# Attention, routed experts and a dense layer on one core: own PSUM for the first queries, gate exponentials moved, expert rows loaded twice, weight quarters in another order

## The chip, the core and the metric

One core of a Trainium2 chip runs the whole program. The metric is device time in microseconds, the median of the timed runs. The engines are named as the profile names them: PE (TensorE matmul), PEld (its weight load), DVE (VectorE), ACT (ScalarE), POOL (GpSimd) and SP (SyncE, which here only issues DMAs). A name with q behind it (SPq, ACTq) is the queue of that engine.

## What is computed

Three stages, each on the result of the one before, all in float32.

- Attention over 8 batches of 8 heads, 576 positions, 64 wide. `phi(x)` projects x to 128 features, subtracts the row's largest absolute value and takes `exp` of plus and minus the result (256 features). Then `num = phi(q) @ (phi(k).T @ v)` and `out = num / (phi(q) @ sum(phi(k)) + 1e-6)`.
- Routed experts over the 4608 tokens of 512. A token with `x @ w_skip <= 0` is passed through. The others go to the expert with the largest of 8 logits `x @ w_gate`; with the softmax weight of that expert, `out = x + gate * (relu(x @ w1[e]) @ w2[e])`, hidden width 1024.
- A dense layer: `h = x @ w_in` (2048 wide), `(h - tanh(h)) @ w_out`.

## The kernel before, in words

**Precision.** Matmuls of the expert and dense layers run in three passes: every operand is split into a high part (an ACT cast, line 96) and a low part (a subtraction, line 97, on DVE or POOL), and high*high, high*low and low*high are added up in PSUM.

**Attention (lines 664 to 796).** The loop over `i` has 32 steps, one for a pair of heads and one half of the positions of two batches. A step projects keys and queries of the next step (`project`, lines 233 to 249, into a PSUM tile `proj` of which the pool `pproj` has a single buffer), `shift`s them on DVE (line 255 reduces, line 259 subtracts, both reading `proj`), exponentiates (`exp_k` on ACT, line 266; `key_sum` adds them up on POOL, lines 278 to 281), transposes the shifted queries (`transpose_q`, line 287, PSUM tile `tq`), exponentiates these (`exp_q`, line 293), and forms key*value (`key_value`, line 306; `key_value_1`, line 320, from the key sums), its copy to SBUF (`keep_key_value`, ACT, line 312) and the numerators (`numerator`, line 344, PSUM tile `num`). As `proj` has one buffer, a projection waits until the `shift` of the projection before it has read the tile. Every engine runs its own instructions in the order in which the code issues them.

Before the loop (lines 664 to 696) step 0's keys and queries are done, with the first of the 16 words of the dense layer's `w_in` in between: `narrow` (line 194) turns a 64-bit word into float32 in four DVE operations and one or two on ACT and POOL (lines 198 to 217), `store_w` puts the result to DRAM, `load_words` loads the next word into the same place. In the loop a word is narrowed over two steps: lines 198 and 201 at the end of an even step, line 210 at the end of the odd one.

Routing runs eight steps behind, in phases (`phase = i % 8`): logits in phase 0, `route_pick` in 1, `route_gate` (lines 439 to 447: ACT exponentiates the logits, line 441, DVE sums them, line 443) and `route_rank` (DVE and POOL) in phase 2 at the end of the step, `route_count` in phase 3 (two small matmuls, then DVE lines 455 and 456).  Phase 2 comes three times in the loop; a fourth `route_gate` runs after it (line 867).

**Experts (lines 864 to 950).** Tokens are scattered to rows `xs` sorted by expert. Three tiles of 128 tokens are done early; the others in a loop whose step handles one tile (16 steps here), from a table `mt` in SBUF. SP reads row numbers, expert numbers and flags out of `mt` into registers (`values_load`, `entry`). A step computes `up` (two halves of the hidden width, each 12 matmuls with `w1`), relu on ACT (line 825), `relu_t` (four transposes and a split into `hh` and `hl`), `xtr(xt)` (the next tile's rows transposed and split into `xTh` and `xTl`), `down` (24 matmuls with `w2`, line 841), `gated` on DVE (line 848) and `out_row`, a store by SP. Three row tiles go round: `xr` holds this tile's rows (read by `gated`), `xt` the next one's (read by `xtr`), `xu` is being loaded; at the end of a step DVE copies `xt` to `xr` and `xu` to `xt` (lines 949 and 950).

Weights of one expert fill `raw[0]` (w1) and `raw[1]` (w2), 2 MB each, loaded by SP in two parts each (`load_part`). In the step where an expert's tiles begin (`first`), `raw[1]` is split in four quarters of 1024 columns (`wsplit(1, ...)`): ACT casts all, DVE subtracts quarters 0 and 2, POOL 1 and 3. Quarters 0 and 1 come ahead of `up(0, 0)`, quarters 2 and 3 right behind it. `down` uses quarter 0 for its first six matmuls, then 1, 2 and 3. In a step whose successor begins an expert (`nfirst`), `raw[0]` is split for the successor (`split_up`, lines 936 to 943). SP loads new weights into a part as soon as its splits have read it: `load_w(..., 1, ...)` at line 928 for `raw[1]`, lines 945 and 946 for `raw[0]`. After the last expert, `raw[0]` takes half of `w_in` in the same way.

**Dense layer (lines 954 to 1066).** Nine blocks of 512 tokens, gathered by indirect DMAs.

Of the kernel before, what the change touches and what calls it, by code (L numbers as in the profile page):

```python
# [8 lines left out]
F32 = mybir.dt.float32  # L9
# [6 lines left out]
PSUM = bass.MemoryType.PSUM  # L16
# [3 lines left out]
P = 128  # L20
# [39 lines left out]
def attention_moe_moe_kernel(  # L60
# [82 lines left out]
    ap = actx.enter_context(tc.tile_pool(name="att", bufs=1))  # L143
    sm = actx.enter_context(tc.tile_pool(name="small", bufs=2))
    pp = actx.enter_context(tc.tile_pool(name="pproj", bufs=1, space=PSUM))
    pt = actx.enter_context(tc.tile_pool(name="ptr", bufs=1, space=PSUM))
    pn = actx.enter_context(tc.tile_pool(name="pnum", bufs=1, space=PSUM))

    kvb = pk.tile([P, 512], F32, name="kvb")

# [6 lines left out]
    kf = [ap.tile([P, 2, 2, NF], F32, name=f"kf{j}") for j in range(2)]  # L157
    qp = [ap.tile([P, 2, NCH, P], F32, name=f"qp{h}") for h in range(2)]
    kvt = ap.tile([P, 2 * NF], F32, name="kvt")
    num = pn.tile([P, 2, 512], F32, name="num")[:, :, : NCH * VE].rearrange("p h (c w) -> p h c w", c=NCH)  # L160

    ko = kvb[:, K_T:].rearrange("p (s h w) -> p s h w", s=2, h=2)
    runb = rt.tile([P, E], F32, name="runb")
# [30 lines left out]
    def narrow(w, e, m, x, dve=False):  # L194

        w = w.rearrange("p (n t) -> p n t", t=2)
        low, high = w[:, :, 0].bitcast(U32), w[:, :, 1].bitcast(U32)
        nc.vector.tensor_scalar(  # L198
            out=e, in0=high, scalar1=0x7FF00000, scalar2=None, op0=ALU.bitwise_and
        )  # L200
        nc.vector.tensor_scalar(  # L201
            out=m, in0=high, scalar1=0xFFFFF, scalar2=None, op0=ALU.bitwise_and
        )
        yield
        nc.scalar.activation(e, e, AF.Relu, scale=8.0, bias=bias[:, 0:1])
        nc.scalar.activation(x, low, AF.Identity, scale=2.0**-32, bias=bias[:, 1:2])  # L206
        if not dve:
            nc.scalar.copy(m.bitcast(F32), m)
        yield
        nc.vector.scalar_tensor_tensor(  # L210
            out=e, in0=high, scalar=0x80000000, in1=e, op0=ALU.bitwise_and, op1=ALU.bitwise_or
        )
        if dve:
            nc.vector.tensor_tensor(out=x, in0=x, in1=m, op=ALU.add)  # L214
        else:
            nc.gpsimd.tensor_tensor(out=x, in0=x, in1=m.bitcast(F32), op=ALU.add)
        nc.gpsimd.tensor_tensor(out=x, in0=x, in1=e.bitcast(F32), op=ALU.mult)  # L217
        yield
# [11 lines left out]
    def blk(c, h):  # L230
        return 4 * h + c if c < 4 else 8 + h

    def project(i, w):


        src = st[i][w]
        p = st[i]["p" + w] = pp.tile([P, 12, NF], F32, name="proj")
        for c in range(4):
            for h in range(2):
                r = slice(h * DH, h * DH + DH)  # L240
                nc.tensor.matmul(
                    p[:, blk(c, h)], src[r, c * P : c * P + P],
                    wpr[r, h * NF : h * NF + NF], start=True, stop=True,
                )
        if tiles(i) == NCH:
            nc.tensor.matmul(
                p[:, 8:10].rearrange("p h f -> p (h f)"), src[:, 4 * P : 5 * P], wpr,
                start=True, stop=True,
            )
# [14 lines left out]
    def exp_k(i, s):  # L264
        d = st[i]["dk"]
        nc.scalar.activation(ke[:, :, s], d[:, :8], AF.Exp, scale=1.0 - 2.0 * s)
        if tiles(i) == NCH:
            for j in range(2):
                q = slice(64 * j, 64 * j + 64)
                nc.scalar.activation(kf[j][q, :, s], d[q, 8:10], AF.Exp, scale=1.0 - 2.0 * s)  # L270
# [165 lines left out]
        )  # L436
        return p, x, oh, cum, nocomp

    def route_gate(p, x, lg, lm, oh):
        ex = rt.tile([P, E, TPP], F32, name="ex")  # L440
        nc.scalar.activation(ex, lm, AF.Exp)
        ssum = rt.tile([P, TPP], F32, name="ssum")
        nc.vector.tensor_reduce(
            out=ssum, in_=ex.rearrange("p e t -> p t e"), axis=AX.X, op=ALU.add
        )
        nc.vector.tensor_scalar_add(ssum, ssum, 1e-9)
        nc.vector.reciprocal(x[:, :, D], ssum)
# [225 lines left out]
    load(2, "k")  # L673
    nc.vector.memset(bias[:, 0:1], -916.0 * 2**23)
    nc.vector.memset(bias[:, 1:2], 2.0**20)
    nc.vector.memset(num[:, :, 4], 1.0)
    for t in kf:
        nc.gpsimd.memset(t, 0.0)
    project(0, "k")
    narrowing = narrow(w_in, *w_tmp)  # L680
    next(narrowing)
    next(narrowing)
    shift(0, "k")
    project(0, "q")
    next(narrowing)
    store_w(0)
    load_words(w_in, 1)
    exp_k(0, 1)
    key_sum(0, 1)
    exp_k(0, 0)  # L690
    key_sum(0, 0)
    shift(0, "q")
    load(1, "v")
    load(2, "q")
    nc.gpsimd.memset(raw[0][:, : 4 * W], 0.0)
    nc.vector.tensor_copy(runb, cst[:, C_EC1 : C_EC1 + E])
    routing = None
# [1 line left out]
    for i in range(NS):  # L699
# [15 lines left out]
            load_part(expert_w(wv), 3)  # L715
        transpose_q(i, 0)
        exp_q(i, 0)
        load(n + 2, "k")
        key_value(i)
        key_value_1(i)  # L720
# [38 lines left out]
        if phase == 1:  # L759
            routing = route_pick(*routing)  # L760
        if phase == 2:
            route_gate(*routing)
            routing = route_rank(*routing)
        if phase == 3:
            route_slot(*routing)
# [38 lines left out]
    with ExitStack() as bctx:  # L804
# [59 lines left out]
        routing = route_pick(*route_logits(NPAIR - 1))  # L864
        wsplit(1, 0, 1024, nc.gpsimd)
        wsplit(1, 1024, 2048, nc.gpsimd)
        route_gate(*routing)
        routing = route_rank(*routing)
        up(0, 0)
        wsplit(1, 2048, 3072, nc.gpsimd)  # L870
# [43 lines left out]
        with tc.For_i(0, ntile, 1, iteration_sync="reg_based") as i:  # L914
            sp, spl = [ET.SP], [ET.Activation, ET.DVE, ET.Pool]
            nxt = nc.values_load(mt[0:1, bass.ds(i + 2, 1)], engines=sp, min_val=0, max_val=RMAX)
            e, more = entry(3, bass.ds(i, 1), E - 1), entry(4, bass.ds(i, 1))
            load_row(xu, nxt)
            first = nc.values_load(mt[2:3, bass.ds(i, 1)], engines=spl, min_val=0, max_val=1)
            nfirst = nc.values_load(mt[2:3, bass.ds(i + 1, 1)], engines=spl, min_val=0, max_val=1)  # L920
            with tc.If(first > 0):
                for j in range(2):
                    wsplit(1, j * 1024, j * 1024 + 1024, nc.gpsimd if j % 2 else nc.vector)
            up(0, 0)
            with tc.If(first > 0):
                for j in range(2, 4):
                    wsplit(1, j * 1024, j * 1024 + 1024, nc.gpsimd if j % 2 else nc.vector)
            load_w(expert_w(e), 1, more)
            e, nlast = entry(3, bass.ds(i + 1, 1), E - 1), entry(5, bass.ds(i + 1, 1))
            more = entry(4, bass.ds(i + 1, 1))  # L930
            dst = nc.values_load(mt[1:2, bass.ds(i, 1)], engines=sp, min_val=0, max_val=NSEG - P)
            p = up(0, 1, range(2))
            relu_t(0, 0)
            up(0, 1, range(2, 4), p)
            xtr(xt)
            with tc.If(nfirst > 0):
                split_up(0, 0, nc.vector)
            y = down(0, range(2))
            relu_t(0, 1)
            with tc.If(nfirst > 0):  # L940
                split_up(0, 2, nc.gpsimd)
                split_up(1, 0, nc.vector)
                split_up(1, 2, nc.gpsimd)
            y = down(0, range(2, 8), y)
            load_w(last_w, 0, nlast)
            load_w(expert_w(e), 0, more)
            gated(y, xr)
            out_row(dst)
            nc.vector.tensor_copy(xr, xt)
            nc.vector.tensor_copy(xt, xu)  # L950
    rctx.close()


# [194 lines left out]
```

## Time and profile before

| | us |
|---|---|
| median of 3 runs (1463.42 to 1468.04) | 1465.85 |
| the profiled execution's own time | 1460.43 |
| its span in the profile | 1458.6 |
| PE busy in the span | 1392.7 (95%) |
| PEld / DVE / ACT / POOL busy | 1150.6 / 701.2 / 555.6 / 388.7 |
| mean granted clock of PE | 0.98 |

The span is the profile's; 1.8 us of the execution lie around it. Attention ends at about 368 us, the loop over the expert tiles takes about 410 to 638 us, and the rest is the dense layer. A busy PE is not a PE at its peak, since matmuls overlap in its pipeline; what PE loses is read from its waits and from the granted clock.

### The profile page before, as it was taken

The page shows a single profiled execution, that of the slowest core. Times are in us where ns is not written, and L with a number is a line of the kernel's source. Part 1 is how long each engine was busy: PE and PEld are TensorE (multiplying, and loading weights), DVE is VectorE, ACT ScalarE, POOL GpSimd, SP SyncE. Part 2 cuts the span into 40 slices and gives each one's busy share as a digit, 9 for nine tenths or more (in the row PEclk, how much of TensorE's full clock was granted, in tenths as well). Part 3 has the DMA queues.
Part 4 walks back from the last instruction along what each step waited for, and adds up shares of the span by engine and source line. Part 5 has one row for each costly group of instructions (what it writes and reads, how often), then busy time and mean ns, then how long its engine had stood idle before and what let it go on. Part 6 is the DMA issues. An engine that isn't in the chain of part 4 may idle for free.

```text
span 1458.6 us, 26066 instructions
## 1 busy us (share of the span) xinstructions
PE 1392.7 (95%) x9733; PEld 1150.6 (79%) x9733; DVE 701.2 (48%) x1083; ACT 555.6 (38%) x910; POOL 388.7 (27%) x413
## 2 busy tenths in 40 slices
PE   6999999988999989859999999999999999999998
PEld 5887887776877878748888888888888888888887
DVE  5788787877735253658852322323223232232322
ACT  4665666565314242536542222223222222222221
POOL 4776887768402020442330100101001010000000
PEclk9999999999999999969999999999999999999999
DMA  5654775946653241443320100101002010000000
GB/s 179 182 182 137 256 247 162 294 157 204 222 174 116 78 151 43 148 171 122 118 99 1 58 1 1 58 0 58 1 1 58 1 58 1 0 30 0 30 1 29
DMA packets 53876, 139.60 MB, mean 96 GB/s; under 512 B 5776, under 2 KB 5904, under 8 KB 50704
## 3 DMA queue, kind: packets, MB, share of 16 engines
q1 hardware_dynamic: 47440, 116.16, 24.3%
q0 software_dynamic: 5760, 18.90, 4.2%
q10 hardware_dynamic: 576, 3.15, 0.6%
q8 instruction: 70, 1.15, 0.3%
q14 instruction: 30, 0.25, 0.1%
HBM read 86.00 MB, written 52.19 MB: 95 GB/s over the span
## 4 chain that ended last, share of the span: by engine, by line
PE 49%; DVE 3%; POOL 2%; ACT 1%; issue 1%; DMA 0%; POOLq 0%
PE h L1015 24%; PE acc L1031 24%; POOL raw L217 1%; PE xtr L1004 1%; DVE wol L97 1%; DVE raw L214 1%; ACT woh L96 1%; DVE raw L210 0%; POOL raw L973 0%; DVE raw L198 0%; DVE wl L97 0%; ACT raw L206 0%; DMA raw<-x2s,gidx 0%; DVE raw L201 0%; DVE g L1019 0%
## 5 line engine op out<-in xcount | busy, mean ns | idle before, releaser
L1019 DVE TENSOR_TENSOR g<-h,g 128x512 f32<-128x512 f32 x144 | 99.4, 691 | 389.8 <-ACT g L1018 389.8
L1018 ACT ACTIVATE g<-h 128x512 f32<-128x512 f32 x144 | 85.7, 595 | 391.7 <-PE h L1015 391.7
L1015 PE MATMUL h<-x2Th,wh 128*128 128x512 f32 (+1 forms) x580 | 226.0, 390 | 0.0
L1015 PE MATMUL h<-x2Tl,wh 128*128 128x512 f32 (+1 forms) x580 | 225.8, 389 | 0.0
L1015 PE MATMUL h<-x2Th,wl 128*128 128x512 f32 (+1 forms) x580 | 225.8, 389 | 0.0
L1031 PE MATMUL acc<-woh,gh 128*128 128x512 f32 x576 | 225.6, 392 | 0.0
L1031 PE MATMUL acc<-woh,gl 128*128 128x512 f32 x576 | 224.3, 389 | 0.0
L1031 PE MATMUL acc<-wol,gh 128*128 128x512 f32 x576 | 224.1, 389 | 0.0
L973 POOL DMA_INDIRECT raw<-x2s,gidx x36 | 35.4, 984 | 428.0 <-PE xtr L1004 416.0
L97 DVE TENSOR_TENSOR gl<-g,gh 128x512 fp32r<-128x512 f32 x144 | 101.1, 702 | 99.0 <-ACT gh L96 99.0
L96 ACT CAST gh<-g 128x512 fp32r<-128x512 f32 x144 | 89.4, 621 | 111.1 <-DVE g L1019 111.1
L1015 PEld LDWEIGHTS h<-x2Th,wh 128*128 128x128 f32 x580 | 110.2, 190 | 22.3
L1015 PEld LDWEIGHTS h<-x2Th,wl 128*128 128x128 f32 x580 | 110.0, 190 | 22.3
L1015 PEld LDWEIGHTS h<-x2Tl,wh 128*128 128x128 f32 x580 | 110.1, 190 | 22.2
L1031 PEld LDWEIGHTS acc<-woh,gl 128*128 128x128 f32 x576 | 108.1, 188 | 22.5
L1031 PEld LDWEIGHTS acc<-wol,gh 128*128 128x128 f32 x576 | 108.2, 188 | 21.9
L1031 PEld LDWEIGHTS acc<-woh,gh 128*128 128x128 f32 x576 | 108.2, 188 | 21.9
L97 POOL TENSOR_TENSOR wl<-raw,wh 128x1024 fp32r<-128x1024 f32 x21 | 56.3, 2708 | 201.0 <-PE y L841 191.1
L344 PEld LDWEIGHTS num<-kv,qp 128*64 128x64 f32 x2304 | 87.7, 140 | 8.6 <-ACT kv L333 7.7
L344 PE MATMUL num<-kv,qp 128*64 128x74 f32 x2304 | 93.0, 235 | 1.1 <-ACT kv L333 0.4
L293 ACT ACTIVATE qp<-tq 128x640 f32<-128x640 f32 (+1 forms) x128 | 76.2, 648 | 46.3 <-PE tq L287 45.0
L841 PE MATMUL y<-wl,hh 128*128 128x512 f32 x152 | 62.5, 411 | 9.4 <-DVE wl L97 9.4
(197 smaller groups left out, 2217.1 us busy)
## 6 DMA issues: line engine op xcount, KB each, us to landing
raw<-in_wall_dram SPq DMA_DIRECT2D x20, 1024.0 KB, 6.3
raw<-in_w_dram SPq DMA_DIRECT2D x30, 512.0 KB, 4.3
x2s<-raw SPq DMA_DIRECT2D x24, 512.0 KB, 6.8
out_dram<-raw SPq DMA_DIRECT2D x36, 256.0 KB, 3.9
x2s<-x SPq DMA_DIRECT2D x9, 768.0 KB, 11.0
k<-in_kT_dram SPq DMA_DIRECT2D x16, 320.0 KB, 4.6
q<-in_qT_dram SPq DMA_DIRECT2D x16, 320.0 KB, 4.8
v<-in_vx_dram SPq DMA_DIRECT2D x16, 320.0 KB, 6.1
```

Source lines behind the costliest of these rows:

```text
L96: nc.scalar.copy(hi, src)
L97: eng.tensor_tensor(out=lo, in0=src, in1=hi.bitcast(F32), op=ALU.subtract)
L214: nc.vector.tensor_tensor(out=x, in0=x, in1=m, op=ALU.add)
L217: nc.gpsimd.tensor_tensor(out=x, in0=x, in1=e.bitcast(F32), op=ALU.mult)
L293: nc.scalar.activation(qp[h][:, s, :n], t[:, :n], AF.Exp, scale=1.0 - 2.0 * s)
L344: nc.tensor.matmul(num[r : r + 64, h, c], qp[h][:, s, slot, r : r + 64], kv[:, s, h], start=s == 0, stop=s == 1,)
L841: nc.tensor.matmul(y, a[:, c, m], b[1][:, m * D : m * D + D], start=m == 0 and a is hh and b is wh, stop=m == 7 and a is hl,)
L973: nc.gpsimd.indirect_dma_start(out=xg[:, t, :], out_offset=None, in_=x2s[:, :], in_offset=bass.IndirectOffsetOnAxis(ap=gidx[:, b * TB + t ...
L1015: nc.tensor.matmul(p[:, s], a[:, o : o + P], b[:, k, s], start=n == 0, stop=n == 11)
L1018: nc.scalar.activation(g, p, AF.Tanh)
L1019: nc.vector.tensor_tensor(out=g, in0=p, in1=g, op=ALU.subtract)
L1031: nc.tensor.matmul(acc[t], a[:, s], b[:, m], start=m == 0 and n == 0, stop=m == NM - 1 and n == 2)
```

## The change

Four edits.

1. Before the loop, step 0's queries are projected into a PSUM pool of their own (`pfirst`), which is closed again before the pools of `tq` and `num` are opened. Keys and queries of step 0 are now shifted, exponentiated and summed first; the first word of `w_in` is narrowed behind them, and the loads of values 1 and queries 2 are issued ahead of that word's store.
2. `route_gate` is cut in two: `gate_exp` (the ACT exponential) is issued in phase 2 right behind `exp_q(i, 0)`, the DVE part stays where it was.
3. In the loop over expert tiles, `xr` is loaded from `xs` at the start of its own step, `xt` right behind `xtr(xt)` for the step after; `xu` is loaded no more there, and the two DVE copies are gone.
4. Quarters 2 and 3 of `raw[1]` are split behind the first half of `up(0, 1)` and `relu_t(0, 0)`, not ahead of them.

```diff
-    def route_gate(p, x, lg, lm, oh):
+    def gate_exp(p, x, lg, lm, oh):
         ex = rt.tile([P, E, TPP], F32, name="ex")
         nc.scalar.activation(ex, lm, AF.Exp)
+        return ex
+
+    def route_gate(p, x, ex):
         ssum = rt.tile([P, TPP], F32, name="ssum")
...
     project(0, "k")
+    with tc.tile_pool(name="pfirst", bufs=1, space=PSUM) as first:
+        project(0, "q", first)
+        shift(0, "k")
+        exp_k(0, 1)
+        key_sum(0, 1)
+        exp_k(0, 0)
+        key_sum(0, 0)
+        shift(0, "q")
+    pt = actx.enter_context(tc.tile_pool(name="ptr", bufs=1, space=PSUM))
+    pn = actx.enter_context(tc.tile_pool(name="pnum", bufs=1, space=PSUM))
...
+    nc.vector.memset(num[:, :, 4], 1.0)
     narrowing = narrow(w_in, *w_tmp)
-    next(narrowing)
-    next(narrowing)
-    shift(0, "k")
-    project(0, "q")
-    next(narrowing)
+    for _ in narrowing:
+        pass
+    load(1, "v")
+    load(2, "q")
     store_w(0)
     load_words(w_in, 1)
-    exp_k(0, 1)
-    key_sum(0, 1)
-    exp_k(0, 0)
-    key_sum(0, 0)
-    shift(0, "q")
-    load(1, "v")
-    load(2, "q")
...
         exp_q(i, 0)
+        if phase == 2:
+            ex = gate_exp(*routing)
...
         if phase == 2:
-            route_gate(*routing)
+            route_gate(*routing[:2], ex)
             routing = route_rank(*routing)
...
-            load_row(xu, nxt)
+            cur = nc.values_load(mt[0:1, bass.ds(i, 1)], engines=sp, min_val=0, max_val=RMAX)
+            load_row(xr, cur)
...
             up(0, 0)
+            p = up(0, 1, range(2))
+            relu_t(0, 0)
             with tc.If(first > 0):
                 for j in range(2, 4):
                     wsplit(1, j * 1024, j * 1024 + 1024, nc.gpsimd if j % 2 else nc.vector)
...
-            p = up(0, 1, range(2))
-            relu_t(0, 0)
             up(0, 1, range(2, 4), p)
             xtr(xt)
+            load_row(xt, nxt)
...
             gated(y, xr)
             out_row(dst)
-            nc.vector.tensor_copy(xr, xt)
-            nc.vector.tensor_copy(xt, xu)
```

## Rows read from the trace of the kernel before

**Rows 1.** Busy time by stretch; x counts instructions, then granted clock, DMA share, GB/s.
```profile
28.00:352.00 324.00, 307.92 (x4655) 258.70 (x4650) 261.57 (x421) 204.79 (x349) 244.72 (x300) 0.98 0.65 201
410.00:638.00 228.00, 211.53 (x962) 168.68 (x960) 108.95 (x115) 80.69 (x117) 48.02 (x18) 0.96 0.34 120
```

**Rows 2.** Timeline of the start: start us, us, engine, line, op [idle before <- releaser].
```profile
6.19 1.22 PE L246 MATMUL proj<-wpr,k 128*128 128x256 f32 x2
...
11.96 2.08 PE L241 MATMUL proj<-wpr,q 64*128 64x128 f32 x16 [4.54 <-issue]
12.60 1.28 POOL L217 TENSOR_TENSOR raw<-raw 128x512 f32<-128x512 f32 x1 [0.76 <-DVE raw L210]
...
16.75 1.49 DVE L259 TENSOR_TENSOR dq<-proj,mq 128x1280 f32<-128x1280 f32 x1
...
19.33 0.73 POOL L281 TENSOR_TENSOR ks<-ks,kf 128x256 f32<-128x256 f32 x1
...
20.36 1.33 PE L287 MATMUL tq<-cst,dq 128*128 128x128 f32 x5
...
24.66 0.58 PE L320 MATMUL kvb<-cst,ks 128*64 128x1 f32 x16
...
28.85 0.61 DVE L198 TENSOR_SCALAR raw<-raw 128x512 uint32<-128x512 uint32 x1
...
32.09 1.49 DVE L255 TENSOR_REDUCE mk<-proj 128x10 f32<-128x1280 f32 x1 [1.75 <-PE proj L246]
```

**Rows 3.** The page's DMA issues: median us from issue to landing is last.
```profile
raw<-in_w_dram SPq DMA_DIRECT2D x30, 512.0 KB, 4.3
```

**Rows 4.** Waits, 20 to 352 us: who <- for whom: total us, times, longest.
```profile
ACT kvt L312 <- PE kvb L320: 45.7, 30, 3.5
...
PE proj L241 <- issue: 6.6, 3, 2.3
...
DVE ssum L443 <- ACT ex L441: 5.1, 3, 1.8
```

**Rows 5.** Busy time by stretch, behind the first of these three waits.
```profile
140.00:150.00 10.00, 9.47 (x110) 8.47 (x111) 5.53 (x10) 3.72 (x8) 5.56 (x8) 0.69 0.24 47
```

**Rows 6.** Timeline of the expert loop: the first relu of five of its steps.
```profile
451.51 0.60 ACT L825 ACTIVATE r<-h 128x512 f32<-128x512 f32 x1 [6.38 <-PE h L820]
...
483.39 0.60 ACT L825 ACTIVATE r<-h 128x512 f32<-128x512 f32 x1 [7.31 <-PE h L820]
...
508.22 0.60 ACT L825 ACTIVATE r<-h 128x512 f32<-128x512 f32 x1 [6.38 <-PE h L820]
...
520.63 0.60 ACT L825 ACTIVATE r<-h 128x512 f32<-128x512 f32 x1 [6.38 <-PE h L820]
...
551.88 0.60 ACT L825 ACTIVATE r<-h 128x512 f32<-128x512 f32 x1 [7.18 <-PE h L820]
```

**Rows 7.** Timeline of a step that begins an expert (about 461 to 480 us).
```profile
463.07 1.79 DVE L949 COPY xr<-xt 128x513 f32<-128x513 f32 x1
...
464.85 1.99 ACT L96 CAST wh<-raw 128x1024 fp32r<-128x1024 f32 x2
...
467.33 4.51 DVE L97 TENSOR_TENSOR wl<-raw,wh 128x1024 fp32r<-128x1024 f32 x2
...
470.76 0.80 PE L841 MATMUL y<-wl,hh 128*128 128x512 f32 x1 [2.34 <-DVE wl L97]
...
472.50 0.79 PE L841 MATMUL y<-wh,hl 128*128 128x512 f32 x1 [0.94 <-DVE hl L97]
```

**Rows 8.** Busy time by stretch, inside the same step.
```profile
472.00:474.00 2.00, 1.50 (x4) 1.22 (x5) 1.04 (x2) 0.00 (x0) 0.00 (x0) 0.50 0.78 268
```

**Rows 9.** SP's queue in the same step: start us, us from first to last issue.
```profile
470.92 1.47 SPq L113 DMA_DIRECT2D raw<-in_wall_dram  x2
```

**Rows 10.** DMA issues of the third such step, 598 to 616 us; landing us last.
```profile
xu<-xs SPq DMA_DIRECT2D x1, 256.5 KB, 4.2
x2s<-yo SPq DMA_DIRECT2D x1, 256.0 KB, 7.3
```

More of the change, by code (lines that the diff above doesn't have):

```diff
@@ L145, in attention_moe_moe_kernel @@
     pp = actx.enter_context(tc.tile_pool(name="pproj", bufs=1, space=PSUM))
-    pt = actx.enter_context(tc.tile_pool(name="ptr", bufs=1, space=PSUM))
-    pn = actx.enter_context(tc.tile_pool(name="pnum", bufs=1, space=PSUM))
     kvb = pk.tile([P, 512], F32, name="kvb")
@@ L159, in attention_moe_moe_kernel @@
     kvt = ap.tile([P, 2 * NF], F32, name="kvt")
-    num = pn.tile([P, 2, 512], F32, name="num")[:, :, : NCH * VE].rearrange("p h (c w) -> p h c w", c=NCH)
     ko = kvb[:, K_T:].rearrange("p (s h w) -> p s h w", s=2, h=2)
@@ L231, in blk, with project @@
         return 4 * h + c if c < 4 else 8 + h
-    def project(i, w):
+    def project(i, w, pool=pp):
         src = st[i][w]
-        p = st[i]["p" + w] = pp.tile([P, 12, NF], F32, name="proj")
+        p = st[i]["p" + w] = pool.tile([P, 12, NF], F32, name="proj")
         for c in range(4):
@@ L675, in attention_moe_moe_kernel @@
     nc.vector.memset(bias[:, 1:2], 2.0**20)
-    nc.vector.memset(num[:, :, 4], 1.0)
     for t in kf:
@@ L679, in attention_moe_moe_kernel @@
     project(0, "k")
-    narrowing = narrow(w_in, *w_tmp)
-    next(narrowing)
-    next(narrowing)
-    shift(0, "k")
-    project(0, "q")
-    next(narrowing)
+    with tc.tile_pool(name="pfirst", bufs=1, space=PSUM) as first:
[8 more added lines that the diff above has]
+    pn = actx.enter_context(tc.tile_pool(name="pnum", bufs=1, space=PSUM))
+    num = pn.tile([P, 2, 512], F32, name="num")[:, :, : NCH * VE].rearrange("p h (c w) -> p h c w", c=NCH)
+    nc.vector.memset(num[:, :, 4], 1.0)
+    narrowing = narrow(w_in, *w_tmp)
+    for _ in narrowing:
+        pass
+    load(1, "v")
+    load(2, "q")
     store_w(0)
     load_words(w_in, 1)
-    exp_k(0, 1)
-    key_sum(0, 1)
-    exp_k(0, 0)
-    key_sum(0, 0)
-    shift(0, "q")
-    load(1, "v")
-    load(2, "q")
     nc.gpsimd.memset(raw[0][:, : 4 * W], 0.0)
@@ L866, in attention_moe_moe_kernel @@
         wsplit(1, 1024, 2048, nc.gpsimd)
-        route_gate(*routing)
+        route_gate(*routing[:2], gate_exp(*routing))
         routing = route_rank(*routing)
```

## The prediction

> **What bounds the kernel now.** I read the busy time by stretch first. From 28 to 352 us PE is busy 307.92 of 324 us, DVE 261.57, POOL 244.72; in the expert loop PE is busy 211.53 of 228 us, DVE 108.95 [rows 1]. So PE sets the end in both stages, and an edit is worth what it gives back to PE: idle time, and time at the lower clock. The dense layer behind them is untouched and only shifts. So the next question is where PE stands still, and that is read from the waits, and then from the timelines around them: the start, three routing steps, and the four steps of the loop that begin new weights (three experts and the half of w_in count as successors; the step itself is seen in rows 7).
>
> At the start, PE finishes step 0's keys at 6.19 + 1.22 = 7.41 us and then stands 4.54 us, because the queries need the same PSUM tile and DVE has the word of w_in ahead of the keys' shift; the shifted queries are there at 16.75 + 1.49 = 18.24 us [rows 2]. In the routing steps DVE waits three times, 5.1 us in all, for the gate exponential, and a projection on PE stands three times for 6.6 us in all (longest 2.3) [rows 4]; it waits for the shift that is queued on DVE behind the gate. In the loop an ordinary step lasts 520.63 - 508.22 = 12.41 us from relu to relu. Two steps of which the second begins an expert last 483.39 - 451.51 = 31.88 and 551.88 - 520.63 = 31.25 us, against 24.82: 7.06 and 6.43 us too long [rows 6].
>
> **The change, part by part.**
>
> *First queries.* PE projects the queries from 7.41 on, for 2.08 + 1.22 = 3.30 us, to 10.7 [rows 2]. DVE no longer has the word ahead: the keys' shift is two operations of 1.49 us, about 7.6 to 10.6, the queries' shift follows to 13.8. It was 18.24: 4.4 us less. The second projection of keys, which stood ahead of the first transposes, now runs in the meantime, since its PSUM tile is free from 10.6 on. So the transposes go from 20.36 to about 13.9, and the matmuls on the key sums, 4.30 us behind them at 24.66, to 18.3 [rows 2]. The key sums on POOL ended at 20.06 (19.33 + 0.73); the two POOL operations of the word (1.28 us each), which held them until 13.88, now stand behind them, so they can start at 11.8 with ACT's first exponentials, and end near 18 [rows 2]. Gain so far 6.2 us.
>
> What is late next is the word. Its POOL part ends at about 18 + 2.6 = 20.6; only then does SP store it and load the next one, behind whose load and store the loads of the loop are queued. These have slack: they serve steps 2 and 3. The next word lands at about 21.2 + 4.3 = 25.5 [rows 3], and line 198, which took it at 28.85, is ready for it at 28.85 - 6.2 = 22.7. DVE would stand 2.8 us, where 1.75 us were free ahead of the next shift [rows 2]; 1.1 us go on to PE. I take 6.2 - 1.1 = **5 us**. Bounds: 6.5 if the word lands in time, 2 if DVE stands as long again (2.8 us) behind another load.
>
> *Gate exponentials.* ACT's 0.3 us go to a place where ACT waits for PE anyway: the copy behind it waits 1.5 us on average (45.7 us in 30 times) [rows 4]. It needs `lm`, which DVE makes in the step before. DVE no longer waits, so the shift, and with it the projection, comes up to 1.7 us earlier each time: **5 us**. PE's waits of 6.6 us bound it, so some 1.5 us remain. Behind one of the three the granted clock was 0.69 for 10 us [rows 5]; if that vanishes, 31% of 10 us, 3.1 us, come on top. The same wait left the clock alone twice, so I don't count it. Bounds 3.5 and 8.
>
> *Copies and row loads.* In ordinary steps the copies lie beside matmuls and cost nothing; the loads that replace them take one more register read on SP and 0.26 MB more per step, hidden by the 12 us until they are used. Were that cover gone, PE would wait for `xt` (a rival below). In a step that begins an expert the copies are dear: the first starts at 463.07 and takes 1.79 us, and only at 467.33 does DVE begin with quarter 0, two subtractions of 4.51 us together. PE stood 2.34 us for that and 0.94 us for the low part of the hidden tile behind it, and its clock fell to 0.50 [rows 7, 8]. Without the copies quarter 0 starts at 463.1 and, even if it alone took all 4.51, ends at 467.6; PE asked at 470.76 - 2.34 = 468.42. That wait goes.
>
> *Weight quarters.* Quarters 2 and 3 are cast behind the split of the hidden tile. So the cast of that tile, which waited for 1.99 us of weight casts until 466.84 [rows 7], comes when its transposes are done, about 466.1, and its low part at 467.4, ahead of quarter 2: the 0.94 us wait goes too. Late next: the second relu, now behind those two casts, at about 468.7 and done at 469.3, just when PE needs it. Up to 0.5 us in each of the four steps. SP has the second half of the old w2 free about 1.5 us later than before; the load has a whole expert's time, save once.
>
> The four steps were too long by 6.75 us on average (the mean of 7.06 and 6.43, taken for all four): 27 us. What I leave in: 4 x 0.5 for the relu; 2 x 1.2 where the successor begins an expert (or w_in) as well, as one more cast of about 1 us then stands ahead of the second hidden half; 1.5 for the one expert with a single tile, whose w2 quarters arrive late, now that the step before is shorter; 3 x 0.5 for `xt`. Together 7.4, say 8. I take **19 us**. Bounds: 27 if nothing is left, 10 if each step keeps a wait as long as today's 2.34 us, with the clock falling again (below).
>
> **The sum.** 5 + 5 + 19 = 29 us. Against the profiled execution (1460.43, span 1458.6) that makes 1431.4. That execution lies 5.4 us below the median of the runs, 1465.85, to which I hold the forecast: 1465.85 - 29 = **1437**.
>
> **A row behind weights.** In the third step of that kind a store of one tile, issued right behind two weight loads of 1 MB, took 7.3 us to land; the row load issued behind it, before the next two weight loads, took 4.2 [rows 10]. The change puts `xt` behind those next two (issued from 470.92 to 472.4 [rows 9]) and some register reads, at about 474.7, and PE wants it at about 480: 5.3 us. At 4.2 it is in time, at 7.3 it is 2 us late; I took 0.5, since the weights are then half through. The Trainium skill ("DMA: Bandwidth & Descriptors", section "Queues, rings and completion order") says that on each DMA engine the descriptors of one issuing queue are consumed in ring order. By that rule the row cannot pass the weights, and the time would be that of rival 2, 1447. The trace agrees for the store with its 7.3 us, and does not for the row with 4.2.
>
> **The rivals.**
>
> 1. *The stall only moves.* The second relu or quarter 3, now last on ACT and POOL, is late by 2.3 us: PE waits as now, and the clock falls as in rows 8. For: ACT's order is tight to 0.1 us by my count. Against: quarter 3 is wanted two quarters after quarter 1. The loop gives back 10 us instead of 19: 1465.85 - 20 = 1446. Chance 0.17.
> 2. *Rows wait for the weights.* If the row starts to move only when the last weights (472.4 + 7.3 = 479.7) are in and then needs its own 4.2, it lands at 483.9, 3.9 us late, at three steps: 11.7 us, less the 1.5 counted: 1447, or a little more if the clock falls. Chance 0.08.
> 3. *More than that.* The clock drops go with the waits, in attention too (3 us), and nothing is left in the loop (8 us): 1426. Chance 0.10.
> 4. *Little moves.* The queries' own tile or the split gate is held by something that I don't see, and the loop keeps its stall: 2 or 3 us. Chance 0.04. Within this lies that an edit doesn't do what it says.
> 5. *Slower: the row replaces the copy as the wait of every step.* `xt` is issued when `xtr` has read it, some 6.4 us into a step (the loads ahead of it on SP included about 7.5), and is wanted 10.9 us later. For PE to lose what the edits give, it would have to wait 29 / 16 = 1.8 us in each of 16 steps, and 2.1 us for a loss that can be told: the row would have to land after 13 us, against the 4.2 of rows 10. At 2.2 us: 1465.85 - 29 + 35 = 1472. Chance 0.03.
>
> The forecast itself has 0.58.
>
> **How the numbers follow.** A measurement of this kernel can tell 0.3%, 4.4 us, from no change. The forecast and rivals 1 to 3 are all faster by more: 0.93. Rival 4 is within, 0.04, rival 5 slower, 0.03. The range: my lowest sums are 2 + 3.5 + 10 = 15.5 (1450), the highest 6.5 + 8 + 27 = 41.5 (1424). I leave out the top few us, where all upper bounds meet, and rivals 4 and 5: 1427 to 1450.
>
> **What would show it.** Right: PE's first transposes at 13 to 15 us; the three waits of DVE for `ex` gone and PE's projection waits below 1 us; steps that begin an expert at 12.4 to 15 us, the 2.34 us waits on quarter 0 gone, the clock at 1.00 there. Wrong: waits of PE on `xt`'s transposes or of the transposes on the row's DMA (rival 2 or 5); waits on the second hidden half or on quarter 3 with the clock at 0.50 (rival 1); DVE standing at line 198 for more than 3 us at 23 us, which would eat the gain of the start.

## The result and the profile after

| | before | after |
|---|---|---|
| median of the runs, us | 1466.94 (1463.42 to 1471.55, 4 runs) | 1452.91 (1451.68 to 1453.31, 4 runs) |
| the profiled execution, us (its span) | 1460.43 (1458.6) | 1453.03 (1451.3) |

The ratio is 0.990, interval 0.9874 to 0.9926: the change is worth 14 us (10.9 to 18.5), half of the forecast 29, and the time lies 3 us above the forecast range. A second set of runs on another occasion (e5 below) gave 1445.83 against 1469.00, ratio 0.9836 (0.9812 to 0.986), so 23 us by the medians; the two intervals do not touch, and that is taken up under "What stays open". The cause is looked for in the traces first, where one stage stands beside the other.

**The start did what was forecast.** PE's timeline of after (start us, us, engine, line, op, [idle before <- releaser]; the line numbers of the attention helpers are lower by three than before), then DVE's:

```profile
7.43 1.16 PE L238 MATMUL proj<-wpr,q 64*128 64x128 f32 x16
...
13.58 0.74 PE L284 MATMUL tq<-cst,dq 128*128 128x128 f32 x5 [1.76 <-issue]
...
18.63 0.63 PE L317 MATMUL kvb<-cst,ks 128*64 128x1 f32 x16 [2.01 <-POOL ks L278]
```

```profile
25.98 0.99 DVE L195 TENSOR_SCALAR raw<-raw 128x512 uint32<-128x512 uint32 x1 [2.19 <-DMA raw<-in_w_dram]
```

They answer to [rows 2]: the 4.54 us of PE ahead of the queries are gone, the first transposes start at 13.58 instead of 20.36 (forecast 13.9), the matmuls on the key sums at 18.63 instead of 24.66 (forecast 18.3), and the next word is what is late then, 2.19 us (forecast 2.8).

**The routing steps lost their wait for the exponential, but not PE's wait.** The waits of after from 20 to 352 us (who <- for whom: total us, times, longest), the same of e2 (the gate edit alone, below), and the busy time of after behind the first routing step (us, busy PE, granted clock, DMA share, GB/s):

```profile
ACT kvt L309 <- PE kvb L317: 36.9, 25, 2.8
...
PE proj L238 <- issue: 5.7, 4, 1.7
```

```profile
PE proj L241 <- issue: 4.0, 3, 1.3
```

```profile
140.00:160.00 20.00, 19.24 (x286) 1.00 0.70 234
```

DVE's wait for the gate exponential [rows 4] is no longer in the list, and the clock of 0.69 behind the first routing step [rows 5] is 1.00. The projection's waits, which I wanted below 1 us, went only from 6.6 to 5.7 us: in the three routing steps 2.2, 2.2 and 2.3 us became 1.3, 1.7 and 1.4, and a fourth of 1.3 us came in step 29.

**The expert loop gained a third of what was forecast.** First relus on ACT around the start of the second expert, three of after, then the one of before that [rows 6] leaves out:

```profile
464.97 0.60 ACT L830 ACTIVATE r<-h 128x512 f32<-128x512 f32 x1 [2.09 <-PE h L825]
...
477.62 0.60 ACT L830 ACTIVATE r<-h 128x512 f32<-128x512 f32 x1 [6.38 <-PE h L825]
...
495.74 0.60 ACT L830 ACTIVATE r<-h 128x512 f32<-128x512 f32 x1 [6.48 <-PE h L825]
```

```profile
464.36 0.60 ACT L825 ACTIVATE r<-h 128x512 f32<-128x512 f32 x1 [2.08 <-PE h L820]
```

The step that begins the expert now takes 477.62 - 464.97 = 12.65 us where it took 483.39 - 464.36 = 19.03; but the step behind it takes 18.12 instead of 12.4. What PE waited for, in the waits from 410 to 640 us, in its timeline, and the busy time around it:

```profile
PE tx L107 <- DMA xt<-xs: 8.5, 3, 3.9
PE y L846 <- DVE hl L97: 2.2, 2, 1.1
PE t L837 <- ACT r L830: 1.7, 1, 1.7
```

```profile
484.67 0.63 PE L107 MATMUL tx<-cst,xt 128*128 128x128 f32 x4 [3.95 <-DMA xt<-xs]
```

```profile
486.00:488.00 2.00, 2.00 (x8) 1.50 (x7) 0.69 (x1) 0.07 (x1) 0.00 (x0) 0.50 0.50 131
```

The 2.34 us on quarter 0 [rows 7] are gone; in their place PE waits 3.95 us for the row in `xt`, and the clock falls to 0.50 behind that wait as it did behind the old one [rows 8]. Why the row is late stands in SP's queue over the same step:

```profile
463.16 2.57 SPq L113 DMA_DIRECT2D raw<-in_wall_dram  x2
466.28 0.35 SPq L861 DMA_DIRECT2D x2s<-yo  x1
473.52 0.34 SPq L103 DMA_DIRECT2D xr<-xs  x1
474.42 1.10 SPq L113 DMA_DIRECT2D raw<-in_wall_dram  x2
478.81 0.34 SPq L103 DMA_DIRECT2D xt<-xs  x1
```

The load of `xt` goes out at 478.81, behind 2 MB of weights. The DMA issues, each from a window of its own around its issue (landing us last), for the tile's store, the second weight load and the row:

```profile
x2s<-yo SPq DMA_DIRECT2D x1, 256.0 KB, 7.1
raw<-in_wall_dram SPq DMA_DIRECT2D x1, 1024.0 KB, 8.7
xt<-xs SPq DMA_DIRECT2D x1, 256.5 KB, 5.7
```

The second weight load, issued at 475.18, lands at 475.18 + 8.7 = 483.9, the row at 478.81 + 5.7 = 484.5, 0.6 us behind it, and PE takes it at 484.67. I had put the row's issue at 474.7. Much of that delay arises between the store of the last tile (466.28) and the load of `xr` (473.52): 7.2 us, where before needed 3.7 for its register reads, by these two lines:

```profile
465.73 0.36 SPq L856 DMA_DIRECT2D x2s<-yo  x1
469.47 0.34 SPq L103 DMA_DIRECT2D xu<-xs  x1
```

The store of after lands at 466.28 + 7.1 = 473.4, and only then does SP go on; its waits from 400 to 645 us:

```profile
SPq L103 <- DMA x2s<-yo: 12.9, 6, 4.8
```

No data passes from the store to the load. The list of SP's instructions with the semaphores they wait for, as the program is built, shows what joins them. (A completion semaphore is the counter that a transfer raises when it has landed; those of the loop are DMAHW0 to DMAHW7, and a transfer that uses one waits for the transfer that used it last.) The loop now holds nine transfers, the eight semaphores are handed out in turn, and the ninth transfer (the store) has that of the first (the load of `xr`). Before, there were eight transfers, and the row's load and the store had one each. After, then before:

```
L103 DMA xr<-xs 128x513 [waits DVE_I-5092_own,DMAHW0_I-5092_own,DMAHW5_49,PE_49]
L861 DMA x2s<-yo 128x512 [waits DMAHW0_I-5092_own,DVE_I-5092_own,DMAHW0_49]

L103 DMA xu<-xs 128x513 [waits DMAHW0_I-5088_own,DVE_I-5088_own]
L856 DMA x2s<-yo 128x512 [waits DMAHW7_I-5088_own,DVE_I-5088_own,DMAHW0_49]
```

**Where the 7.3 us of the span come from.** The expert loop starts at 413.75 instead of 414.26 (its first relu): 0.5. From there to the dense layer's first transposes it takes 226.57 instead of 232.61: 6.0. The rest, 0.8, lies behind. So in this one pair of executions nearly all that the start and the routing steps had gained is lost again in steps 25 to 29 of attention: for example the granted clock from 285 to 300 us is lower (us, busy PE, granted clock, DMA share, GB/s; after, then before):

```profile
285.00:300.00 15.00, 12.82 (x157) 0.77 0.50 159
...
285.00:300.00 15.00, 12.40 (x163) 0.89 0.60 159
```

Two things had to be told apart by runs: whether the wait for `xt` really is what eats the loop's gain, and whether attention's loss belongs to the edits.

### The profile page after: what moved, and what is told of

It is laid out like the page before. It is cut to its first block, busy times and chain, and to the rows that moved or that the text cites. A ratio compares the mean times of both kernels' runs of the same rounds, so it can differ in the third digit from the quotient of the medians.

```text
span 1451.3 us, 26117 instructions
## 1 busy us (share of the span) xinstructions
PE 1385.4 (95%) x9733; PEld 1144.3 (79%) x9733; DVE 676.3 (47%) x1051; ACT 555.4 (38%) x910; POOL 390.9 (27%) x413
## 4 chain that ended last, share of the span: by engine, by line
PE 49%; DVE 3%; POOL 2%; ACT 1%; issue 1%; DMA 0%; POOLq 0%
PE h L1020 24%; PE acc L1036 24%; POOL raw L214 1%; PE xtr L1009 1%; DVE wol L97 1%; DVE raw L211 1%; ACT woh L96 1%; POOL raw L978 0%; DVE raw L207 0%; DMA raw<-x2s,gidx 0%; DVE raw L195 0%; DVE wl L97 0%; ACT raw L203 0%; DVE raw L198 0%; DVE g L1024 0%
## 5 line engine op out<-in xcount | busy, mean ns | idle before, releaser
L341 PE MATMUL num<-kv,qp 128*64 128x74 f32 x2304 | 96.2, 238 | 5.5 <-ACT kv L330 2.9
L263 ACT ACTIVATE ke<-dk 128x1024 f32<-128x1024 f32 x64 | 67.9, 1060 | 12.2 <-DVE dk L256 8.5
```

Source lines behind the costliest of these rows:

```text
L341: nc.tensor.matmul(num[r : r + 64, h, c], qp[h][:, s, slot, r : r + 64], kv[:, s, h], start=s == 0, stop=s == 1,)
```

## The experiments

Each kernel was timed beside runs of before on the same chip; e1 to e4, e5 to e8 and e9 to e12 shared theirs, each of the three on an occasion of its own. All traces are read by the same marks: the copy `kvt` of attention's steps 11 and 31, the first relu of the loop, the loop from there to the dense layer's first transposes, and what follows. Times of one profiled execution each, us; the ratio is the estimate from all runs of the two kernels, with its interval; it can differ from the quotient of their medians, by 0.0017 in e9.

| kernel | kvt 11 | kvt 31 | first relu | loop | behind | ratio to before |
|---|---|---|---|---|---|---|
| before | 136.54 | 364.01 | 414.26 | 232.61 | 811.7 | |
| after | 132.42 | 362.39 | 413.75 | 226.57 | 811.0 | 0.990 (0.9874 to 0.9926) |
| e1: first queries | 131.35 | 354.24 | 404.69 | 232.50 | 810.4 | 0.9955 (0.9935 to 0.9974) |
| e2: gate | 136.15 | 362.04 | 412.79 | 233.42 | 812.4 | 0.9951 (0.9929 to 0.9973) |
| e3: loop's edits | 136.83 | 370.32 | 418.79 | 224.74 | 810.7 | 0.9902 (0.9879 to 0.9925) |
| e4: row ahead | 133.84 | 358.36 | 406.83 | 213.32 | 811.2 | 0.9809 (0.9784 to 0.9834) |
| e5: after again | 131.60 | 357.23 | 408.17 | 225.26 | 810.7 | 0.9836 (0.9812 to 0.986) |
| e6: six transfers | 131.61 | 357.34 | 410.29 | 218.69 | 813.5 | 0.9859 (0.9834 to 0.9884) |
| e7: quarters | 135.76 | 366.25 | 419.18 | 221.41 | 811.8 | 0.991 (0.9885 to 0.9934) |
| e8: rows | 135.44 | 368.59 | 419.38 | 220.68 | 811.0 | 0.9895 (0.987 to 0.992) |
| e9: row ahead again | 131.57 | 356.37 | 410.59 | 214.61 | 811.4 | 0.9827 (0.9805 to 0.985) |
| e10: queries and gate | 131.89 | 353.96 | 407.02 | 233.35 | 812.1 | 0.9928 (0.991 to 0.9945) |
| e11: loop, row ahead | 135.14 | 372.54 | 424.08 | 214.49 | 811.8 | 0.9879 (0.9854 to 0.9905) |
| e12: row ahead, one load | 132.43 | 359.49 | 413.25 | 215.23 | 811.0 | 0.9813 (0.9791 to 0.9835) |

**e1, the first queries alone.** Before with the change's edits of the start.

```diff
-    project(0, "q")
+    with tc.tile_pool(name="pfirst", bufs=1, space=PSUM) as first:
+        project(0, "q", first)
...
-    next(narrowing)
+    for _ in narrowing:
+        pass
```

> The kernel before with only the first queries in PSUM of their own (and the word, its store and the loads behind them). In the trace of after the start is 4.1 us ahead, and at the end of attention 0.5 us of all attention gains is left. Theory A (what is lost in steps 25 to 29 hangs on when those steps come, not on an edit): the 4.1 us of the start stand in the first steps here too, and how much of it arrives is open, between nothing and all: -4 to 0 us against before. Rival B (the gate edit causes the loss by making other instructions late): the 4 us arrive here whole, -4 +/- 0.5 us (ratio 0.997), and the relu that opens the expert loop comes at 410 instead of 414.26 us.

Measured: 1452.44 against 1460.61, -8.2 by the medians and -6.6 by the ratio (-3.8 to -9.5). The step-11 copy is 5.2 us early. Theory A allowed for no more than the start's 4 and is missed upward, rival B's 4 lie within the interval; but the first relu, 404.69, is 5 us earlier than B had it. This execution also lacks the clock drop that before has near 290 us (1.00 against 0.89 from 285 to 300 us), but 11% of 15 us is less than 2. One execution's attention doesn't tell an edit's worth.

**e2, the gate exponentials alone.**

```diff
+        if phase == 2:
+            ex = gate_exp(*routing)
...
-            route_gate(*routing)
+            route_gate(*routing[:2], ex)
```

> The kernel before with only the gate exponentials moved. Theory A: the waits for the gate exponential go in all three routing steps; the first site, whose clock drop goes too, gives 3 to 4 us, the others 0.5 to 1 each, 4 to 5 us in all by step 24; if steps 25 to 29 come at another time than in after, the gain may arrive, -3 to -5 us against before. Rival B (the gate edit itself makes steps 25 to 29 late): the gain is gone by step 29 as in after, -1 to +1 us, and the stalls at the third routing step and two steps behind it stand here as in after.

Measured: 1453.41, -7.2 us (-3.9 to -10.4). The gain arrives in the runs, so the edit doesn't lose it in steps 25 to 29; B falls. The profiled execution is the longest of its seven (1460.42) and shows a gain of 1.5 us only at the first relu.

**e3, the two edits of the loop alone.**

```diff
-            load_row(xu, nxt)
+            load_row(xr, cur)
...
+            load_row(xt, nxt)
...
+            p = up(0, 1, range(2))
+            relu_t(0, 0)
...
-            nc.vector.tensor_copy(xr, xt)
-            nc.vector.tensor_copy(xt, xu)
```

> The kernel before with only the two edits of the expert loop. Attention stands as in before. Both theories of the loop (the row waits for SP and the weights; or the new order of casts is late) expect what after gained behind 408 us: -6 us, +/- 1.5 (ratio 0.995 to 0.997), with PE waiting three times for xt, some 8 us in all. If the gain is much larger here, the loss of xt in after hung on when the loop began.

Measured: 1446.81, -14.3 us by the ratio (-11 to -17.7), more than the 6 expected. The trace has the loop at 224.74, 7.9 us below before, with the three waits for `xt` (6.8 us). That execution is the longest of its eight (1440.12 to 1456.02); what the median has beyond its 7.9 us no trace shows.

**e4, the row ahead of the weights.** After, with one pair of lines exchanged on SP's queue.

```diff
-            load_w(expert_w(e), 1, more)
...
             xtr(xt)
             load_row(xt, nxt)
+            load_w(expert_w(e), 1, more)
```

> After, with the row load for xt issued ahead of the second pair of weight loads on SP's queue instead of behind them. Nothing else is changed. Theory C (the row is late because it stands behind 2 MB of weights and SP is late): xt is issued near 475 instead of 478.81 us, lands in 3 us, ahead of PE's need at 480.7; PE's waits for xt (8.5 us in 3 times) go, the clock doesn't fall behind them, and the steps of 18.12, 17.76 and 16.47 us become 12.5 to 14: 9 to 13 us less than after, about 1441, ratio 0.982 to 0.985 to before. Rival D (the new order of casts is what is late, the row only the last to be seen): the wait moves to the second relu or quarter 3, less than 3 us gained on after. Rival E (bandwidth: row and weights share the same engines, so the w2 quarters are now late instead): PE or ACT waits for raw, less than 5 us gained.

Measured: 1433.04, ratio 0.9809: 28 us below before. SP's queue in the step that begins the second expert:

```profile
458.29 0.36 SPq L861 DMA_DIRECT2D x2s<-yo  x1
464.91 0.34 SPq L103 DMA_DIRECT2D xr<-xs  x1
465.52 0.33 SPq L103 DMA_DIRECT2D xt<-xs  x1
466.40 1.10 SPq L113 DMA_DIRECT2D raw<-in_wall_dram  x2
```

and the first relus of the same steps:

```profile
456.93 0.60 ACT L830 ACTIVATE r<-h 128x512 f32<-128x512 f32 x1 [2.08 <-PE h L825]
...
469.58 0.60 ACT L830 ACTIVATE r<-h 128x512 f32<-128x512 f32 x1 [6.38 <-PE h L825]
...
481.99 0.60 ACT L830 ACTIVATE r<-h 128x512 f32<-128x512 f32 x1 [6.38 <-PE h L825]
```

SP still waits for the store (`xr` goes out 6.6 us behind it), but `xt` goes out 0.6 us behind `xr` and lands in 2.8 us, 4 us before PE wants it. The steps take 12.65 and 12.41 us, and no wait for `xt` is left in the list. The loop stage is 213.32, 13.3 us below after. By the trace theory C stands, D and E fall; after itself was not timed on this occasion. One step misses what C said, the last, 16.30 us: there the w2 of the expert with a single tile arrives late, as the forecast had it, and the relu stands behind its casts:

```profile
599.36 0.63 PE L837 MATMUL t<-cst,r 128*128 128x128 f32 x4 [1.58 <-ACT r L830]
```

**e5, after once more.** No edit.

> After once more, unchanged, beside the same runs of before as the others of this call. Theory A (clock drops in attention fall at other places from execution to execution; no edit causes those of steps 25 to 29): the relu that opens the expert loop comes at another time than 413.75, anywhere from 406 to 414 us, while the loop from the first relu to the last takes 204 +/- 2 us again, because the three waits for xt are of its making. Rival B (the stalls of steps 25 to 29 belong to the code): 413.5 to 414 again, with the same two stalls near 326 and 338 us. Time to before: ratio 0.990 again by both.

Measured: 1445.83, ratio 0.9836. The first relu comes at 408.17, 5.6 us earlier than in the other execution of the same program, and the clock that was 0.77 is full:

```profile
285.00:300.00 15.00, 12.37 (x198) 1.00 0.56 181
```

The loop, with its three waits for `xt`, is there again (first relu to last 202.85, expected 204 +/- 2). So the stalls of steps 25 to 29 don't belong to the code. Rival B falls, and A's ratio of 0.990 is missed as well.

**e6, six transfers in the loop.** After, with each pair of weight loads as one; the row stays behind them.

```diff
-            for a in (2 * j, 2 * j + 1):
-                load_part(src, a)
+            nc.sync.dma_start(raw[j], src(slice(j * 4096, j * 4096 + 4096)))
```

> After, with each pair of 1 MB weight loads of the loop issued as one load of 2 MB, so that the loop holds six transfers instead of nine; the row load for xt stays behind the second of them. Theory F (the first row load waits for the landing of the store of the step before because the two share a completion semaphore, as the instruction list shows of the nine; the wait makes SP late): with six transfers the row load doesn't wait for the store any more, it is issued 3.5 instead of 7.2 us after it in the steps that begin an expert; xt goes out 3 to 4 us earlier but still lands behind the 2 MB, near the time PE wants it: PE's waits for xt fall from 8.5 us to 0 to 3 us in all, and the kernel is 6 to 12 us below after. Rival G (only the place behind the weights matters): the weights end when they end, xt still lands as late, less than 3 us gained.

Measured: 1448.33, 2.5 us above after beside it, the intervals overlap. SP's queue in the step that begins the second expert, and PE's wait:

```profile
461.91 0.36 SPq L860 DMA_DIRECT2D x2s<-yo  x1
465.94 0.34 SPq L103 DMA_DIRECT2D xr<-xs  x1
467.52 0.34 SPq L118 DMA_DIRECT2D raw<-in_wall_dram  x1
471.10 0.34 SPq L103 DMA_DIRECT2D xt<-xs  x1
```

```profile
478.17 0.63 PE L107 MATMUL tx<-cst,xt 128*128 128x128 f32 x4 [2.05 <-DMA xt<-xs]
```

Theory F's mechanism is right: the wait for the store is gone from SP's list, `xr` goes out 4.0 instead of 7.2 us behind it, and PE waits 2.1 us for `xt` in all instead of 7.0 (e5); the loop stage is 6.6 us shorter than in e5. (e6 also makes one load of each pair, so the semaphore is not all that differs.) Its time is wrong: the dense layer takes 813.5 instead of 810.7 in this execution, and the first relu comes 2.1 us later; what of that belongs to the edit isn't known. Rival G is half right too. The issues of the second weight load and of the row behind it:

```profile
raw<-in_wall_dram SPq DMA_DIRECT2D x1, 2048.0 KB, 9.8
xt<-xs SPq DMA_DIRECT2D x1, 256.5 KB, 6.9
```

The weights land at 467.52 + 9.8 = 477.3, the row at 471.10 + 6.9 = 478.0, right behind them as in after. The row is less late because the weights are: they go out 5.6 us behind the store, in after 8.1.

**e7 and e8, one edit of the loop at a time.** e7 has the order of the quarters without the row loads, e8 the row loads without that order; each is one part of the diff of e3.

```diff
             up(0, 0)
+            p = up(0, 1, range(2))
+            relu_t(0, 0)
             with tc.If(first > 0):
```

> Before with the new order of the weight quarters alone: the copies of the row tiles and the early load of the row into xu stay. Theory C (in after the row load is what is left): here no row is late. DVE still copies for 1.8 us ahead of quarter 0, but the hidden tile's casts don't queue behind weight casts and PE's 0.94 us go; of the 2.34 us on quarter 0 at most half stay. The four long steps lose 2 to 6 us each: 10 to 20 us below before, ratio 0.986 to 0.993. Rival D (the new order makes the second relu or quarter 3 late): less than 6 us below before.

Measured: 1455.04, ratio 0.991, -13.2 us, as theory C had it. The steps that begin an expert take 15.05 and 15.03 us. DVE's copies still stand ahead of quarter 0, whose subtraction starts only at 472.21:

```profile
467.98 1.78 DVE L949 COPY xr<-xt 128x513 f32<-128x513 f32 x1
469.79 2.50 DVE L950 COPY xt<-xu 128x513 f32<-128x513 f32 x1
472.21 1.21 DVE L97 TENSOR_TENSOR wl<-raw,wh 128x1024 fp32r<-128x1024 f32 x1
```

```diff
-            load_row(xu, nxt)
+            load_row(xr, cur)
...
+            load_row(xt, nxt)
...
-            nc.vector.tensor_copy(xr, xt)
-            nc.vector.tensor_copy(xt, xu)
```

> Before with the row loads alone (no copies, xt loaded behind the second pair of weights), in the old order of the quarters. Theory C: quarter 0 starts 1.8 us earlier at the four steps and PE's 2.34 us shrink to about 0.5, 2 to 3 us each with the clock; against this stand three waits for xt of 2 to 4 us with the clock down behind them, 10 to 13 us in all: between 5 us faster and 6 us slower than before. Rival D (the order of the casts is what costs, the row comes in time where the step before is long): no wait for xt, 6 to 10 us faster.

Measured: 1453.93, ratio 0.9895, -15.4 us. Both ranges are missed: I had priced the copies too low and the row too high. The steps that begin an expert take 13.97 and 13.94 us, 1.3 us longer than in after, and the row is nearly in time: PE waits for it 3.0 us in all. So each edit alone shortens the loop stage by some 12 us, and both together (e3, after) by 6 to 8. That the shorter step is what makes the row late fits this, but no run varied the step's length alone.

**e9 to e12** ran together. e9 is the kernel of e4; e10 is before with e1's and e2's edits; e11 is e3 with e4's exchange; e12 is e4 with the pair of w2 loads as one:

```diff
-            load_w(expert_w(e), 1, more)
+            with tc.If(more > 0):
+                nc.sync.dma_start(raw[1], expert_w(e)(slice(4096, 8192)))
```

> The kernel with the row load ahead of the weights once more, to stand beside the three others of this call. Ratio 0.981 +/- 0.003 to before; first relu to last in the loop 192 +/- 1 us, with no wait of PE for xt.

> Before with the first queries and the gate exponentials, and the loop as it was. Theory A (attention's edits add up, and only clock drops that fall by chance hide it in one execution): -6.6 and -7.1 us were measured for the two alone, so -9 to -14 us, ratio 0.990 to 0.994. Rival B (together they lose to each other, as the profile of after has it with 0.5 us): less than 5 us, ratio above 0.9965.

> Before with the two edits of the loop and the row load ahead of the weights, attention as in before. Theory C: what the loop's edits are worth without the wait for xt, the 19 us of the prediction or a little less: -15 to -20 us, ratio 0.986 to 0.990, where the two loop edits with the row behind the weights gave -14; first relu to last 192 +/- 1 us instead of 206. Rival (the -27.6 us of the whole lay in attention): no more than -14.

> The kernel with the row ahead of the weights, in which the pair of w2 loads behind it is one load of 2 MB, so that the loop holds eight transfers and the first row load shares no completion semaphore with the store. Theory F of the semaphore: SP's waits of the row load for the store's landing (9.6 us in 5 times) go, xr is issued 3.5 to 4 instead of 6.6 us after the store in the steps that begin an expert. The time: the row had some 4 us to spare already, and w2 is late only for the expert with one tile (1.6 us): 0 to -2 us against the kernel with two loads. Were it more than 2 us faster, SP's lateness would still cost something that I don't see; were it slower, the one load that lands as a whole comes too late for the casts.

Measured, with differences of medians: e9 1442.16 (ratio 0.9827), first relu to last 192.39 us, no wait of PE for `xt`: as expected. e10 1457.96, -12.1 us (-10.6 by the ratio): A stands, attention's edits add up. e11 1452.21, -17.8 us, first relu to last 192.35: C stands. The sum of e10 and e11 is 29.9 us, the whole (e9) 27.9. e12 1441.20, 1 us below e9, as expected: SP's waits for the store are gone, `xr` goes out 4.5 us behind it (expected 3.5 to 4), and the time hardly moves: in e4 the row had 4 us to spare.

The version to keep is that of e4: 1433.04 against 1460.61, 1442.16 against 1470.02, and in the loop stage 213.3 to 214.6 us against 224.7 to 226.6 in three executions each. The timed runs show less of a difference than the loop stage: the ratios are 0.9809 and 0.9827 with the row ahead, 0.990 and 0.9836 with it behind, never side by side. e12 is no worse.

## Why the prediction was wrong

**The step that failed** is "3 x 0.5 for `xt`" in the sum, with its reason in "A row behind weights". In the traces the wait for the row cost 11.4 us of the loop stage: 214.14 us on average with the row ahead of the weights (e4, e9, e11) and 225.52 with it behind them (after, e5, e3). Two things in that step were wrong.

1. *The issue.* "at about 474.7" was taken from before's SP queue [rows 9] plus some register reads. The row went out at 478.81: `xr`, put ahead of the weights, became the ninth transfer's partner in a semaphore and held SP until the last tile's store had landed, and that store itself stands behind 2 MB of weights (7.1 us here, 7.3 in [rows 10]). So the weights ahead of the row went out 8.1 us behind the store instead of 470.92 - 465.73 = 5.2. I counted the added load as one more register read and never asked what it waits for. In e6, where SP doesn't wait for the store, the wait for `xt` goes from 7.0 to 2.1 us.
2. *The landing.* I read the 4.2 us of the row in [rows 10] as a row that had not waited for what stood ahead of it. SP's queue of before at that place shows the misreading:

```profile
600.20 2.57 SPq L113 DMA_DIRECT2D raw<-in_wall_dram  x2
603.33 0.35 SPq L856 DMA_DIRECT2D x2s<-yo  x1
607.08 0.34 SPq L103 DMA_DIRECT2D xu<-xs  x1
```

That store landed at 603.33 + 7.3 = 610.6 and that row at 607.08 + 4.2 = 611.3, behind it: its time was short because it went out late, not because it passed anything. The row of the change, behind a pair of weight loads, did the same: in after, e3, e5, e6 (there one load of 2 MB) and e8 it stood so 20 times, and each time it landed 0.6 to 1.0 us behind the last of the weights and 8.0 to 10.5 us behind the issue of the first. Ahead of them it took 2.8 (e4). The Trainium skill ("DMA: Bandwidth & Descriptors", section "Queues, rings and completion order") says that each DMA engine consumes the descriptors of one issuing queue in ring order. The traces agree with it in all 20 cases, and for the row with 4.2 too, which the prediction held against it.

Rival 2, to which I gave 0.08, is what happened in kind. That its price, 11.7 us, is so near the 11.4 is luck. It had the row 3.9 us late at three steps; PE waited 0.9, 3.9 and 3.6 us, and the clock added the rest, as the steps are 1.1, 5.7 and 5.4 us longer than 12.4. It had the row take 4.2 us of its own behind the weights where it needed 0.6, and the weights go out as early as before, which they did not.

**The other terms, on average over executions.**
- *Loop without that wait: 19 us forecast.* The stage is 232.97 us where the loop is as before (before, e1, e2, e10) and 214.14 with the row ahead: 18.8. The waits on quarter 0 are gone, the second relu costs 12.65 - 12.41 = 0.24 us a step (0.5 allowed), the late w2 of the single-tile expert makes PE wait 1.6 to 2.2 us (1.5).
- *First queries: 5 us.* The step-11 copy comes at 135.98 on average in six executions without the edit and at 132.09 in eight with it: 3.9. The mechanism was right, word included. (The prediction's own times give 24.66 - 18.3 = 6.4 where it says 6.2; the trace has 6.0 at that place.)
- *Gate: 5 us.* From the step-11 to the step-31 copy: 230.8 us on average in six executions without (222.9 to 237.4), 225.7 in eight with it (222.1 to 230.0): 5.1, by means of groups that overlap. The size came out, but not by the mechanism: PE's three waits in the routing steps, which were to go but for 1.5 us, are 4.4 us of 6.6 in after and 4.0 in e2, so they gave 2 to 3. What still holds the projection there is open. About half of the gain came from the first routing step, with its clock, which I had left out of the sum: step 12, from copy to copy, takes 12.5 us in seven of the eight executions with the edit (15.3 in e2) and 14.9 to 16.2 in the six without. That the two errors cancel is luck.

With 7.4 (232.97 - 225.52) in place of 19, and the other two as measured, the sum is 3.9 + 5.1 + 7.4 = 16.4. The two measurements, 14 and 23, lie on both sides of it.

**What stays open.** First, what the wait for the row costs in timed runs. It is 13 us between after and e4, but only 1 us by the ratios, or 5 by the medians, between e5 and e9, and 3 to 4 between e3 and e11 (the loop's edits alone). On the one occasion of e1 to e4 the parts alone (e1, e2 and e3, the row behind the weights) sum to 6.6 + 7.2 + 14.3 = 28.1 us by their ratios, as much as the 27.9 of e4, the whole with the row ahead. The 11.4 us are shown in the loop stage of six traces; the medians don't confirm them, and no trace shows why.

Second, why after gave 14 us on one occasion and 23 on another. The granted clock goes with it: 0.982 to 0.984 in the four runs of after, 0.983 to 0.988 in the five of e5, 0.9825 and 0.9864 on average. As an estimate, 0.4% of 1450 us is 6 of the 7 us between their medians; why the clock differs isn't shown. The prediction took 4.4 us as what a measurement can tell; the same change measured twice differs by 9. The medians of before differ as well, 1460.61 to 1470.02 on four occasions. The first relu of seven executions of kernels with both attention edits lies between 406.83 and 413.75, of five without them between 414.26 and 424.08. The pair of executions that I read first was the earliest of the one kind and the latest of the other: 0.5 us apart, where the averages are 9.1 us apart.

## What to carry to other kernels

A transfer that is moved behind others on its queue is to be priced from *their* landing, not from the time that a like transfer took elsewhere: read when each landed, not how long it took. A small load that is wanted soon goes ahead of large ones that are wanted late, which here took one exchange of lines and shortened the loop stage by 11 us. One more transfer in a loop isn't free because its bytes are few: look at which semaphore it gets and what then waits for what. And where a step is shortened, ask for every transfer in it whether it was in time only because the step was long: e7 and e8 each gave 13 to 15 us, both together (e3) 14.

## What the runs showed of the hardware

- A row of 0.26 MB issued behind 2 MB of weights on the same queue landed 0.6 to 1.0 us behind the last of them in 20 cases (after, e3, e5, e6, e8), 8.0 to 10.5 us behind the issue of the first; ahead of them it took 2.8 (e4).
- The clock of one and the same program differs from execution to execution: 0.77 and 1.00 from 285 to 300 us in two executions of after, whose first relus lie 5.6 us apart. Over seven executions of kernels with the same attention edits that relu spreads over 6.9 us, so a stage-by-stage difference of two single traces is no measure for an edit worth 5 us.
